# Heads of a sliding-window attention: scores and maxima twelve steps ahead of the exponentials instead of ten

## The chip, the cores and the metric

The kernel runs on one core of one Trainium2 chip. The metric is the device time of one execution in microseconds (us), the median of three runs. A core has a matrix engine (TensorE, PE in the profile; its weight loads are PEld), VectorE (DVE), ScalarE (ACT), GpSimd (POOL) and SyncE (SP), which here issues every DMA, in order. Matrix products land in PSUM, eight banks of 512 fp32 columns on 128 partitions.

## The reference, cut to what matters

Four layers, attention, Fourier mixing, attention, Fourier mixing, each on the normalised running sum `x` (2048 rows, 640 columns). The change touches the two attention layers alone:

```python
H = 32; Dh = D // H; W = 256
qkv = (x @ wqkv).reshape(B, S, 3, H, Dh).transpose(2, 0, 3, 1, 4)
q, k, v = qkv[0], qkv[1], qkv[2]
scores = einsum("bhqd,bhkd->bhqk", q, k) * (Dh ** -0.5)
mask = (idx[:, None] - idx[None, :] >= 0) & (idx[:, None] - idx[None, :] < W)
p = softmax(where(mask, scores, -1e9), axis=-1)
o = einsum("bhqk,bhkd->bhqd", p, v)
return o.transpose(0, 2, 1, 3).reshape(B, S, D) @ wo
```

A query sees its own block of 128 keys and the two before it, so a block row of scores is at most 384 wide.

## The kernel before, in words

**Before the heads** (`before_heads`, L368) the layer's rows are normalised and transposed, the value projections are made and stored, and the first two of ten column chunks of the query and key projection are done. A chunk is 128 columns: 6 or 7 heads' worth of rows of either kind. The other eight chunks are made *inside* the head loop, as filler for PE.

**The head loop** (`heads`, L606) walks 32 heads as 8 quads of 4 heads, each with 16 blocks of 128 queries: 128 steps. In a loop step three stages stand at different places of this sequence:

- `s = step + LEAD`: *scores and maxima*. `s_head` (matmul L631, DVE reduction L636) makes one block row of scores for one head and takes its masked row maximum, four times a step. Every fourth `s`, `m_rows` (L641) transposes the maxima of four blocks (PE, L644), negates them on ACT into `mt` (L647), and two DMAs (L649) write them as an extra row of `qp`.
- `t = step`: *exponentials*. `t_pair` (L659) makes the transposed scores again, now with the extra row, so that the maximum is already subtracted; `t_exp` (ACT, L669) takes the exponential and `t_mask` (POOL, L675 and L679) cuts the corners.
- `v = step - 1`: *values*. `pv` (L694) multiplies by V, three key blocks of four heads, and ACT copies the result out (L701). Every fourth `v`, `finish` (L705) posts, so many half steps later: the DMA that gathers the row sums (`sm`, L711), the store of the output rows (`o_d`, L712), the DVE reciprocal (L714) and the store of the reciprocals (`r_d`, L717).

A half step is one turn of the loop `for z in range(2)`; `post(delay, ...)` counts those. PSUM banks 0 to 3, and from step -1 also 4 and 5, go round among the three stages (`ring6`); 6 and 7 belong to the filler.

**The filler** is `fill(n)` (L752), which draws about `n` units from `project` (L568), a unit being two matmuls L257 of 512 columns that run side by side on two halves of the rows. 480 units are to be made in each layer. With `lead` on (steps below -2) and up to step -1 the filler is called in both half steps, `FIRST` units each; later once a step, `RATE` = 4 units. A piece of 128 by 512 results takes 15 units with its partner: pieces are made in sets of two banks, a first half of the rows and then the other half, and between the halves DVE reads a column of both banks (`seen`, L263) so that no two row halves write a bank at once. When a set is finished, ACT copies its banks out (L544), POOL splits the copy into two parts, and a DMA (L524) stores them in `qk_d`. In the leading steps a chunk is made as one group of four banks, 6, 7, 4 and 5, two sets side by side, and the copies are called at once.

After the last chunk the filler makes the first part of the output projection (`partials`, L954) out of chunks of `o_d` and `r_d` that `load_o` (L839) fetches and scales: 16 row blocks, some 18 units each, `LATE` = 9 units a step. `load_y` (L949) fetches the rows of `x` that are added.

**Order of the loads.** `due` (L726) holds for each quad `q` and quarter `j` the `s` at which `pack` (L582) is called; its twelve DMAs (L594, `kp` and `qp` from `qk_d`, 80 KB each) go out three a step over four steps. SP issues in program order, and a DMA that has to wait holds up all behind it. Loads are therefore counted from `s`, the finishing of quads and the filler's second part from `v` and `t`.

Of the kernel before, what the change touches and what calls it, by code (L numbers as in the profile page):

```python
# [21 lines left out]
NQ = H // 4  # L22
# [4 lines left out]
SCALE = DH ** -0.5  # L27
EPS = 1e-5

LEAD = 10  # L30
AHEAD = 8
EARLY = 3
AHEAD_X = 4
AFTER = 4
RATE = 4
FIRST = 7
LATE = 9
BACK = 2
PACE = 0.65
# [25 lines left out]
class Net:  # L65
# [501 lines left out]

    def project(self):  # L568
        for c in range(2, NCH):
            lead = self.lead  # L570
            for sbs in ((0, 1, 2, 3),) if lead else ((0, 1), (2, 3)):
                if sbs[0] == 0 and c > 2:
                    self.load_chunk(c + 1)
                if sbs[-1] == 3:
                    self.cut_chunk(c + 1)
                if c == NCH - 1:
                    self.prepare(sbs[0])
                yield from self.pieces(c, sbs, "f" if lead else "m")
        self.prepare(4)
# [26 lines left out]
    def heads(self, xsrc, xdst, hook):  # L606
# [78 lines left out]
        def pv(quad, qb, bank):  # L685

            bk, at = qb // 4, qb % 4 * P
            if qb % 4 == 0:
                ous[quad, bk] = self.next("ou")
            for kb in range(max(qb - 2, 0), qb + 1):  # L690
                t = pt[quad, kb]
                vq = self.vq[(4 * quad + kb // 4) % 3]
                for h in range(4):
                    nc.tensor.matmul(  # L694
                        self.banks[32 * h:32 * h + 32, bank, :P],
                        vq[:, 96 * (kb % 4) + 21 * h:96 * (kb % 4) + 21 * h + 32],
                        t[:, h, (qb - kb) * P:(qb - kb + 1) * P],
                        start=kb == max(qb - 2, 0), stop=kb == qb,
                        tile_position=(0, 32 * h), skip_group_check=True)
            pt.pop((quad, qb - 2), None)  # L700
            nc.scalar.activation(ous[quad, bk][:, at:at + P], self.banks[:, bank, :P], AF.Copy)  # L701
            if qb % 4 == 3:
                finish(quad, bk)

        def finish(quad, bk):  # L705
            ou = ous.pop((quad, bk))
            sm = pool.tile([P, 16], F32, name="sm", tag="sm")
            rc = pool.tile([P, 16], F32, name="rc", tag="rc")
            cols = slice(bk * 512, (bk + 1) * 512)
            at = (2, 9, 11) if quad < NQ - 1 else (1, 5, 6)  # L710
            self.post(at[0], lambda: nc.sync.dma_start(sm, ou[0:P:32, :]))  # L711
            self.post(at[0], lambda: nc.sync.dma_start(  # L712
                self.od[4 * quad:4 * quad + 4, :, cols].rearrange("h r s -> (h r) s"), ou))
            self.post(at[1], lambda: nc.vector.reciprocal(out=rc, in_=sm))  # L714

            def store():
                nc.sync.dma_start(  # L717
                    self.rd[bk, 4 * quad:4 * quad + 4, :].rearrange("h (a b) -> (h a) b", b=16), rc)
                self.post(2 if quad < NQ - 1 else 0, lambda: self.stored.add((quad, bk)))
            self.post(at[2], store)  # L720
# [55 lines left out]
        self.ring6 = dict.fromkeys((0, 1, 2, 3), -99.0)  # L776
        for step in range(-LEAD, steps + 1):
            now[0] = self.step = step
            clock = step * STEP
            if step == -1:  # L780
                self.ring6.update({4: -99.0, 5: -99.0})
            if step + LEAD == steps + 1:
                for b in ROLES["w"]:
                    self.ring6.pop(b, None)
            self.wide, self.lead, self.tiled = step + LEAD > steps, step < -2, step < steps - 1
            for f in later.pop(step, []):
                f()
            s, t, v = step + LEAD, step, step - 1
            if due and s >= due[0][0]:
# [9 lines left out]
            if done[0] < total:  # L799
                nf = max([FIRST if t < -2 else RATE + (t < 0)]  # L800
                         + [(d - done[0]) / max(1, at - s) for at, d, _, _ in due])
# [37 lines left out]
    def load_o(self, o, sb, k, raw=None, rr=None):  # L839
# [46 lines left out]

        busy = self.step + LEAD < 16 * NQ
        n, lane, eng = (2, "pool", nc.gpsimd) if busy else (1, "dve", nc.vector)
# [977 lines left out]
```

## Time and profile before

| | |
|---|---|
| median of three runs | 2188.04 us (2186.35 to 2188.07) |
| the profiled execution, whole | 2187.93 us |
| its span, first to last instruction | 2186.2 us |
| head loop of the first attention layer | about 125 to 530 us of the span |
| head loop of the second | about 1217 to 1619 us |
| PE, DVE, ACT, POOL busy over the span | 97%, 73%, 52%, 44% |

The page gives sums over the whole program; the head loops are two fifths of it, so stretches of them are read by the view that sums busy time in windows. The number of instructions L669 in a window tells how many steps it holds, two for each. A granted PE clock of 1.00 is full speed. PE's share of busy time says little there: ends of matmuls are modelled, and a waiting matmul can look long.

### The profile page before, as it was taken

To read this page: it belongs to the slowest core of one execution; us is meant where nothing else is said; L and a number is where in the kernel's file an instruction comes from. 1 tells how busy PE (TensorE), PEld (TensorE's weight loads), DVE (VectorE), ACT (ScalarE), POOL (GpSimd) and SP (SyncE) were. 2 spreads that over 40 slices of the span, in tenths; PEclk is the share of its full clock that TensorE was granted. 3 is DMA by queue.
4 is the path that set the end of the run, shared out by engine and by line. 5 is a ranking of instruction groups with operands and counts; after the bars stand their busy time and mean duration, and the time that the engine had idled before them with its cause. 6 is when DMAs were issued, how large, how long until landed. Compare 5 with 4: busy or idle time off the path is not lost.

```text
span 2186.2 us, 48927 instructions
## 1 busy us (share of the span) xinstructions
PE 2118.1 (97%) x17872; PEld 1783.2 (82%) x17872; DVE 1603.7 (73%) x3931; ACT 1140.5 (52%) x2125; POOL 958.0 (44%) x1562
## 2 busy tenths in 40 slices
PE   7999999988999999999999999999899999999999
PEld 7987777677878888889999877776778888888899
DVE  6358888886897868786661588888767968677676
ACT  3117777656554545452341177777565645445332
POOL 3037776765614222322430377767655033231324
PEclk9999999999999999999999999999999999999999
DMA  5546666785555354656645556567855454546653
GB/s 183 175 157 190 198 180 215 211 224 169 202 192 189 127 183 141 214 177 207 207 156 167 162 186 200 181 212 226 216 161 182 140 182 132 174 152 208 222 165 125
DMA packets 227089, 398.40 MB, mean 182 GB/s; under 512 B 39969, under 2 KB 86561, under 8 KB 226849
## 3 DMA queue, kind: packets, MB, share of 16 engines
q1 hardware_dynamic: 226848, 395.28, 57.3%
q8 instruction: 141, 2.31, 0.5%
q14 instruction: 100, 0.81, 0.1%
HBM read 273.94 MB, written 120.06 MB: 180 GB/s over the span
## 4 chain that ended last, share of the span: by engine, by line
PE 78%; DVE 7%; DMA 5%; ACT 4%; issue 3%; POOL 2%; SPq 1%; ACTq 0%; DVEq 0%; POOLq 0%
PE banks L1416 29%; PE banks L239 15%; PE banks L257 12%; PE banks L694 6%; PE banks L659 5%; PE banks L1704 5%; PE banks L631 5%; DMA qp<-qk_d 2%; DVE banks L636 1%; ACT pt L669 1%; DMA x_d<-x 1%; PE banks L341 1%; DMA kp<-qk_d 1%; ACT big L1039 1%; DVE qp L232 1%
## 5 line engine op out<-in xcount | busy, mean ns | idle before, releaser
L636 DVE CUSTOM_DVE_ANT_0 banks<-banks,mask 128x384 f32<-128x384 f32 (+2 forms) x1024 | 527.6, 557 | 123.0 <-PE banks L631 99.9
L669 ACT ACTIVATE pt<-banks 128x768 f32<-128x768 f32 (+2 forms) x512 | 393.8, 772 | 168.7 <-PE banks L659 55.2
L675 POOL TENSOR_SCALAR_AFFINE_SELECT pt<-pt 128x256 f32<-128x256 f32 x512 | 213.3, 417 | 213.8 <-ACT pt L669 192.0
L257 PE MATMUL banks<-big,wc 64*128 64x512 f32 x1920 | 271.1, 394 | 0.4 <-DVE pt L442 0.4
L659 PE MATMUL banks<-qp,kp 61*128 61x384 f32 (+2 forms) x1024 | 210.2, 381 | 22.8 <-DVE mc L636 17.4
L694 PE MATMUL banks<-pt,vq 128*32 128x128 f32 x5760 | 211.6, 278 | 3.5 <-ACT pt L669 3.4
L631 PE MATMUL banks<-kp,qp 60*128 60x384 f32 (+2 forms) x1024 | 205.5, 347 | 6.7 <-DVE mc L636 3.1
L257 PEld LDWEIGHTS banks<-big,wc 64*128 64x128 f32 x1920 | 186.8, 185 | 22.6 <-ACT x L544 1.5
L679 POOL TENSOR_SCALAR_AFFINE_SELECT pt<-pt 128x256 f32<-128x256 f32 x448 | 193.8, 433 | 0.0
L226 ACT ACTIVATE qp<-pt 128x512 fp32r<-128x512 f32 (+1 forms) x200 | 123.2, 625 | 128.1 <-DVE pt L1347 51.7
L232 DVE TENSOR_TENSOR qp<-pt,qp 128x512 fp32r<-128x512 f32 (+1 forms) x198 | 156.6, 798 | 42.1 <-ACT qp L226 40.5
L694 PEld LDWEIGHTS banks<-pt,vq 128*32 128x32 f32 x5760 | 142.4, 110 | 51.5 <-issue 35.3
L659 PEld LDWEIGHTS banks<-qp,kp 61*128 61x128 f32 x1024 | 108.0, 184 | 87.3 <-DVE mc L636 65.2
L1416 PE MATMUL banks<-qp,big 128*128 128x512 f32 x648 | 152.9, 390 | 0.0
L631 PEld LDWEIGHTS banks<-kp,qp 60*128 60x128 f32 x1024 | 123.6, 186 | 31.9 <-DVE mc L636 16.4
L1345 POOL TENSOR_TENSOR pt<-pt,pt 128x512 f32<-128x512 f32 x32 | 47.2, 1475 | 231.4 <-DMA pt<-c 173.4
L226 ACT ACTIVATE c<-pt 128x512 fp32r<-128x512 f32 x146 | 90.4, 625 | 111.1 <-POOL pt L1325 57.1
L636 DVE DVE_READ_ACCUMULATOR2_ANT mc<- 128x1 f32 x1024 | 145.0, 142 | 0.0
L1416 PEld LDWEIGHTS banks<-qp,big 128*128 128x128 f32 x648 | 120.8, 188 | 24.2
L232 DVE TENSOR_TENSOR c<-pt,c 128x512 fp32r<-128x512 f32 x144 | 113.8, 793 | 26.9 <-ACT c L226 24.4
L1416 PE MATMUL banks<-qp,xc 128*128 128x512 f32 x480 | 117.4, 391 | 4.3 <-DVE xc L232 2.8
L552 POOL CAST c<-x 128x512 fp32r<-128x512 f32 x64 | 38.9, 611 | 166.5 <-ACT x L544 162.3
(253 smaller groups left out, 4479.9 us busy)
## 6 DMA issues: line engine op xcount, KB each, us to landing
pt<-c SPq DMA_DIRECT2D x166, 512.0 KB
qk_d<-c SPq DMA_DIRECT2D x80, 512.0 KB
kp<-qk_d SPq DMA_DIRECT2D x384, 80.0 KB
qp<-qk_d SPq DMA_DIRECT2D x384, 80.0 KB
kp<-u_d SPq DMA_DIRECT2D x32, 640.0 KB
o_d<-ou SPq DMA_DIRECT2D x64, 256.0 KB
x_d<-x SPq DMA_DIRECT2D x48, 320.0 KB
v_d<-pt SPq DMA_DIRECT2D x16, 768.0 KB
```

The source lines that it names most:

```text
L226: nc.scalar.activation(hi, src, AF.Copy, scale=-1.0 if neg else 1.0)
L232: (eng or nc.vector).tensor_tensor(out=lo, in0=src, in1=hi.bitcast(F32), op=OP.subtract)
L239: self.nc.tensor.matmul(p, x, y, start=n == 0, stop=n == last)
L257: self.nc.tensor.matmul(ps[a], x[r], y[r], start=half + i == 0, stop=half == 1 and i == n - 1, skip_group_check=True)
L631: nc.tensor.matmul(p, qp[quad % 2][b:b + 60, z, qb * P:(qb + 1) * P], kp[quad % 2][b:b + 60, z, k0 * P:(qb + 1) * P], start=True, stop=True)
L636: nc.vector.tensor_tensor_reduce(out=p, in0=p, in1=self.mask[:, 384 - n * P:], scale=1.0, scalar=NEG, op0=OP.add, op1=OP.max, accum_out=mc ...
L659: nc.tensor.matmul(self.banks[:, banks[e], :n * P], kp[quad % 2][b:b + 61, z, kb * P:(kb + 1) * P], qp[quad % 2][b:b + 61, z, kb * P:(kb + ...
L669: nc.scalar.activation(pt[quad, kb][:, 2 * z:2 * z + 2, :n * P], self.banks[:, b0:b1 + 1, :n * P], AF.Exp, scale=SCALE)
L675: nc.gpsimd.affine_select(out=t[:, :, 0:P], in_=t[:, :, 0:P], pattern=[[0, 2], [1, P]], compare_op=OP.is_ge, fill=0.0, base=0, channel_mul ...
L679: nc.gpsimd.affine_select(out=t[:, :, 256:384], in_=t[:, :, 256:384], pattern=[[0, 2], [-1, P]], compare_op=OP.is_gt, fill=0.0, base=0, ch ...
L694: nc.tensor.matmul(self.banks[32 * h:32 * h + 32, bank, :P], vq[:, 96 * (kb % 4) + 21 * h:96 * (kb % 4) + 21 * h + 32], t[:, h, (qb - kb) ...
L1416: nc.tensor.matmul(self.banks[:, bk, :], p, b[q], start=start and m == 0, stop=stop and last and m == 2, skip_group_check=True)
```

## The change

Four edits, of numbers and conditions alone.

```diff
-LEAD = 10
+LEAD = 12
-FIRST = 7
+FIRST = 5
...
     def project(self):
         for c in range(2, NCH):
-            lead = self.lead
+            lead = self.lead and c == 2
             for sbs in ((0, 1, 2, 3),) if lead else ((0, 1), (2, 3)):
...
-            at = (2, 9, 11) if quad < NQ - 1 else (1, 5, 6)
+            at = (1, 5, 6) if quad == NQ - 1 else (2, 9, 11) if (quad, bk) == (NQ - 3, 0) else (2, 12, 14)
```

The loop starts at step -12 and the scores run twelve steps ahead of the exponentials; the ten leading steps with `lead` on take some 10 units each, where eight took 15. By the program's own counting the projection stands at 235 units at step 0, against 255, and ends with step 96 instead of step 91. The partials begin one step later (98 against 97) and fourteen of them are done by step 126 against 125; at the loop's end both stand alike. Only chunk 2 is made as a group of four banks; chunk 3, made in the lead as well, goes by sets of two on banks 6 and 7. Reciprocals and their stores are posted 12 and 14 half steps behind `finish` instead of 9 and 11, but for the last quad and one quarter of the sixth, which keep theirs.

What this moves, first on ACT from the start of the head loop of the first attention layer (`wc` are split weights of the next chunk, `x` the copied-out projections, `mt` the negated maxima). Before:

```order
L219 ACTIVATE wc<-x 128x384
L219 ACTIVATE wc<-x 128x256
L544 ACTIVATE x<-banks 128x512 x4
L219 ACTIVATE wc<-x 128x384
L219 ACTIVATE wc<-x 128x256
L647 ACTIVATE mt<-banks 16x128
L544 ACTIVATE x<-banks 128x512 x4
L647 ACTIVATE mt<-banks 16x128
```

And now, up to the first exponentials:

```order
L219 ACTIVATE wc<-x 128x384
L219 ACTIVATE wc<-x 128x256
L544 ACTIVATE x<-banks 128x512 x2
L647 ACTIVATE mt<-banks 16x128
L544 ACTIVATE x<-banks 128x512 x2
L647 ACTIVATE mt<-banks 16x128
L544 ACTIVATE x<-banks 128x512 x2
L219 ACTIVATE wc<-x 128x384
L219 ACTIVATE wc<-x 128x256
L669 ACTIVATE pt_95<-banks 128x768
L544 ACTIVATE x<-banks 128x512
```

The third pair of copies (step -4) empties banks 6 and 7 while the next set, which needs the same two banks, is the very next filler.

In the steady steps ACT's `mt` copy changes place against the pairs of L544. Before, steps 10 and 11 of the same layer:

```order
L669 ACTIVATE pt_97<-banks 128x768 x2
L701 ACTIVATE ou_99<-banks 128x128
L647 ACTIVATE mt<-banks 16x128
L669 ACTIVATE pt_98<-banks 128x768
L544 ACTIVATE x<-banks 128x512
L669 ACTIVATE pt_98<-banks 128x768
L544 ACTIVATE x<-banks 128x512
L701 ACTIVATE ou_99<-banks 128x128
```

Now, step 8:

```order
L701 ACTIVATE ou_100<-banks 128x128
L669 ACTIVATE pt_95<-banks 128x768
L544 ACTIVATE x<-banks 128x512
L669 ACTIVATE pt_95<-banks 128x768
L544 ACTIVATE x<-banks 128x512
L701 ACTIVATE ou_100<-banks 128x128
L647 ACTIVATE mt<-banks 16x128
```

The maxima go out at steps 0, 4, 8 where they went at 2, 6, 10, so that every second time they share the step with both copies of a set.

Last, SP where the first quarter of the last quad is loaded (`kp_104` and `qp_105` from `qk_d`; `big` are rows of `x`, `x<-o_d` and `rr` chunks for the partials). Before, from step 96:

```order
L594 DMA kp_104<-qk_d 20x2x512 x3
L952 DMA big_5880<-x 128x640
L859 DMA x<-o_d 128x1x512
L865 DMA rr_103<-r_d 128x1x512
L859 DMA x<-o_d 128x1x512
L711 DMA sm<-ou_100 128x1x16
L712 DMA o_d<-ou_100 128x512
L717 DMA r_d<-rc 128x16
L594 DMA qp_105<-qk_d 20x2x512 x3
```

Now, from step 94:

```order
L594 DMA kp_104<-qk_d 20x2x512 x6
L717 DMA r_d<-rc 128x16
L594 DMA qp_105<-qk_d 20x2x512 x3
L621 DMA vq_93<-v_d 128x384
L649 DMA qp_106<-mt 2x4x128 x2
L594 DMA qp_105<-qk_d 20x2x512 x3
L952 DMA big_6085<-x 128x640
L711 DMA sm<-ou_100 128x1x16
L712 DMA o_d<-ou_100 128x512
```

The loads of that quarter now all stand ahead of the fetches for the partials; those of the next quarter have the fetches among them.

## The prediction

> **What bounds the kernel now.** I read the page first, then the two head loops by windows, then how many steps each window holds, last the waits inside.
>
> ```profile
> span 2186.2 us, 48927 instructions
> PE 2118.1 (97%) x17872; PEld 1783.2 (82%) x17872; DVE 1603.7 (73%) x3931; ACT 1140.5 (52%) x2125; POOL 958.0 (44%) x1562
> ```
>
> The profiled execution took 2187.93 us, 1.7 more than its span and 0.1 under the median of 2188.04; sums below start from 2187.93. PE looks full over the whole program, so I ask stage by stage. Windows of the head loops (columns: length, busy us and count of PE, PEld, DVE, ACT, POOL, clock, DMA share, GB/s): the eight leading steps, steps -2 and -1, the steady steps, and the same for the second attention layer.
>
> ```profile
> 125.50:156.50 31.00, 30.81 (x275) 25.45 (x277) 19.21 (x73) 4.24 (x9) 11.54 (x17) 1.00 0.43 138
> 156.50:161.30 4.80, 4.80 (x44) 3.71 (x42) 3.90 (x14) 1.35 (x3) 3.47 (x6) 1.00 0.67 239
> 161.30:413.50 252.20, 247.78 (x3491) 188.04 (x3489) 209.89 (x786) 184.81 (x337) 184.52 (x423) 1.00 0.64 196
> 1217.40:1247.90 30.50, 30.50 (x275) 26.41 (x273) 19.35 (x73) 4.25 (x10) 11.60 (x17) 1.00 0.44 140
> 1247.90:1252.60 4.70, 4.70 (x42) 3.61 (x42) 3.84 (x14) 1.35 (x3) 3.42 (x6) 1.00 0.66 242
> ```
>
> In the lead PE has no idle time and DVE, at 19 of 31, has plenty: the lead is PE's. Its inside, from the timeline of PE:
>
> ```profile
> 148.63 0.34 PE L631 MATMUL banks<-kp,qp 60*128 60x384 f32 x2
> 148.81 1.99 PE L257 MATMUL banks<-big,wc 64*128 64x512 f32 x16
> 150.64 0.34 PE L631 MATMUL banks<-kp,qp 60*128 60x384 f32 x2
> 150.82 1.77 PE L257 MATMUL banks<-big,wc 64*128 64x512 f32 x14
> 152.42 0.34 PE L631 MATMUL banks<-kp,qp 60*128 60x384 f32 x2
> ```
>
> A half step with 8 units (16 matmuls) and two scores takes 150.64 - 148.63 = 2.01, one with 7 units 1.78. So a unit costs 0.23 us and two scores 0.17. A step of 15 units is 3.79.
>
> Then the steps after the lead, by exponentials (ACT L669, busy us and count; two make a step):
>
> ```profile
> 161.30:413.50 252.20, 143.12 (x184) 1.00 0.64 196
> 413.50:428.50 15.00, 6.38 (x10) 0.79 0.68 212
> 428.50:502.00 73.50, 32.74 (x42) 1.00 0.79 217
> 502.00:523.05 21.05, 11.21 (x14) 1.00 0.51 154
> 523.05:527.05 4.00, 2.58 (x4) 1.00 0.63 199
> 1252.60:1504.80 252.20, 143.18 (x184) 1.00 0.63 197
> 1504.80:1518.00 13.20, 6.41 (x10) 1.00 0.81 251
> 1518.00:1591.20 73.20, 32.74 (x42) 1.00 0.82 215
> 1591.20:1612.05 20.85, 11.32 (x14) 1.00 0.40 121
> 1612.05:1616.05 4.00, 2.58 (x4) 1.00 0.64 201
> ```
>
> Steady steps, 3.75 units on average: 252.2 / 92 = 2.74. Five steps without any filler (projection done, partials not ready): 13.2 / 5 = 2.64 in the second layer. So four units, 0.92 us of PE work, cost a step 0.1: the filler hides under the chain of scores, DVE maxima and banks. Steps with 9 units and scores: 73.2 / 21 = 3.49; with 9 and no scores 20.85 / 7 = 2.98; with neither 2.0. **A unit is dear in the lead and nearly free in the middle**, and that is the difference the change works on.
>
> **The change part by part.**
>
> *Lead.* Before, the ten steps below 0 took 31.0 + 4.8 = 35.8 and 30.5 + 4.7 = 35.2. Their work is 135 units (120 to 255) and 20 pairs of scores: 31.05 + 3.4 = 34.45; some 1.05 is left over for the start and the two transposes of the maxima. Now 115 units and 24 pairs: 26.45 + 4.1 + 1.05 = 31.6. DVE does not become the bound:
>
> ```profile
> 125.50:161.30 35.80, 20.23 (x77) 1.00 0.46 151
> ```
>
> That is all L636 work of the lead, 40 scores at 0.51, or 2.0 us a step against 2.64 for 10 units and four scores on PE.
>
> Against it stands chunk 3 on two banks. Its second set starts in the half step after its first ends, and must wait for both copies.
>
> ```profile
> L544 ACT ACTIVATE x<-banks 128x512 f32<-128x512 f32 x24 | 14.4, 600 | 0.1
> L647 ACT ACTIVATE mt<-banks 16x128 fp32r<-16x128 f32 x23 | 5.8, 252 | 0.1
> L669 ACT ACTIVATE pt<-banks 128x768 f32<-128x768 f32 (+2 forms) x184 | 143.1, 778 | 52.0 <-PE banks L631 18.3 <-POOL pt L675 17.8 <-PE banks L659 9.3
> ```
>
> Two copies are 1.2, less the 0.17 of scores that PE has meanwhile: 1.0. Two changes of row halves wait for DVE's column read between half steps, from nothing to two reductions (1.0) each. Taken 0.15 each, since DVE is idle a quarter of the time; the ends are 0 and 3.0 for all of it. The copies before stood behind other banks and cost nothing. Lead now 31.6 + 1.3 = 32.9: **-2.6 a layer, -5.2 in all** (ends -7.8 and -1.8).
>
> *Middle.* By the second layer: before 252.2 + 13.2 + 73.2 + 20.85 + 4.0 = 363.45. Now 97 steps of 2.74, one empty with scores, 18 of 3.49, ten of 2.98, one of 2.0: 265.8 + 2.6 + 62.8 + 29.8 + 2.0 = 363.0. The twenty units that left the lead fill five steps that were empty, which costs 0.1 a step; two steps of 9 units lose their scores, which pays for it. **-0.5 a layer, -1.0.**
>
> *The clock.* The first layer's empty steps took 15.0, the second's 13.2.
>
> ```profile
> 421.00:429.00 8.00, 7.27 (x72) 4.96 (x72) 5.35 (x20) 3.98 (x10) 4.01 (x8) 0.58 0.81 269
> 1512.00:1520.00 8.00, 7.27 (x107) 5.03 (x98) 6.95 (x26) 4.64 (x11) 5.04 (x11) 1.00 0.94 296
> ```
>
> Same place, same code, but a clock of 0.58 in the first. The stretch is where PE has least to do, and it shrinks from five steps to one. I take the drop as gone: **-1.8** (ends -2.3, the whole difference of the two layers' middles, 365.75 - 363.45, and 0).
>
> [...]
>
> *DMA waits.* Idle before an instruction of PE stands in brackets:
>
> ```profile
> 432.08 0.45 PE L659 MATMUL banks<-qp,kp 61*128 61x384 f32 x2 [1.08 <-DMA qp<-mt]
> 446.68 0.29 PE L631 MATMUL banks<-kp,qp 60*128 60x128 f32 x1 [1.00 <-DMA kp<-qk_d]
> 1536.29 0.29 PE L631 MATMUL banks<-kp,qp 60*128 60x128 f32 x1 [2.05 <-DMA qp<-qk_d]
> ```
>
> The first is a step whose exponentials waited for the maxima; two more steps between them make that wait go. The other two are the first scores of the last quad, whose loads stood behind the fetches for the partials; now they are issued ahead of them. The loads of the quarter behind get the fetches instead, so half is taken: 4.1 in all, **-2.0** (ends -4.1 and, a like wait for the quarter behind, +4.1).
>
> *Crowding and reciprocals.* Two more groups, of the whole program:
>
> ```profile
> L701 ACT ACTIVATE ou<-banks 128x128 f32<-128x128 f32 x256 | 71.5, 279 | 61.2 <-PE banks L694 49.9 <-DMA kp<-qk_d 0.4
> L714 DVE RECIPROCAL rc<-sm 128x16 f32<-128x16 f32 x64 | 15.9, 248 | 2.7 <-DMA sm<-ou 2.7
> ```
>
> Maxima, the finishing of a quarter and the first loads of a pack now begin in the same step, every fourth. ACT in a steady step has 2 x 0.78 + 0.28, a step with a set's copies 3.0, and with `mt` besides 3.3 against a step of 2.74. If the extra 0.25 shows each time (12 sets a layer) it is +6; if two delays that stood apart overlap, as much comes back. ACT is busy 185 of 252, so most of it is absorbed: taken **+2** (ends -6 and +6).
>
> The reciprocals cost 248 ns each, as many as before, and DVE waits 2.7 us for their sums in the whole program; they are moved behind a later phase of the same queue. The store of a quarter's reciprocals is wanted only by the fetches for the partials, and the one that the first partial waits for keeps its delays: nothing.
>
> Sum: -5.2 - 1.0 - 1.8 - 2.0 + 2.0 = -8.0, or **2179.9**.
>
> **The rivals.**
>
> *The clock drop stays* (0.12): all else as above, -6.2, 2181.7.
>
> *The lead's gain is eaten* (0.22): set changes cost 3.0 a layer instead of 1.3 (+3.4), the last quad's loads wait as before (+2), crowding takes 2 more and the clock stays low half the time: about -1, 2187. For it: in the lead a set change has no step of pv and exponentials to hide under. Against it: DVE and ACT are far from full there.
>
> *Slower by crowding* (0.16): one mechanism, in every fourth steady step. The transpose of the maxima holds PE's queue, and pv, the scores and all filler stand behind it. In the lead such a half step takes 1.76 us (157.53 to 159.29) where its neighbour takes 1.32:
>
> ```profile
> 157.53 0.34 PE L631 MATMUL banks<-kp,qp 60*128 60x384 f32 x2
> 159.29 0.34 PE L631 MATMUL banks<-kp,qp 60*128 60x384 f32 x2
> 160.61 0.34 PE L631 MATMUL banks<-kp,qp 60*128 60x384 f32 x2
> ```
>
> That is 0.44 for maxima that now share the step with a set's copies and the start of the loads. If 0.3 more is lost in each of 24 such steps in each layer, that is +14.4, and -8.0 becomes +6.4: 2194. It decides from 8.0 / 48 = 0.17 us a step.
>
> *Everything overlaps* (0.12): crowding gives back 4 instead of taking 2: 2174.
>
> **How the numbers follow.** The forecast itself has 0.38, its own range 2176.5 to 2183.5. A measurement of this kernel can tell about 0.2%, 4.4 us, from no change. The forecast, the staying clock and the overlap are faster by more: 0.62. The eaten gain is the same: 0.22. Crowding is slower: 0.16. The range reaches down to a little under the overlap and up to half of the slower case: 2172 to 2190.
>
> **What would show it.** The lead's window would be 32 to 34 us from the first scores to step 0, with PE gaps of about a microsecond at one set change behind ACT L544. The five steps without filler would shrink to one, with the clock at 1.00 in the first layer too. The waits of 1.0 and 2.05 before the last quad's first scores would be smaller. Steady steps would stay at 2.70 to 2.78; at 2.85 or more, with waits for ACT or for DVE at every fourth step, the crowding rival is right. A lead of 35 us would refute the first term, and with it the prediction.

## The result, and the profile after

The changed kernel takes **2192.75 us** (median of 13 runs, 2189.99 to 2197.61) against 2186.7 for the kernel before in the same session: 1.0029 times as long, 95% interval 1.0019 to 1.0039. It is slower by 0.3%, where the prediction had 2179.9 and faster. The profiled execution took 2191.20 us, 3.3 more than the 2187.93 of before.

The page's head says nothing of where: every engine is as busy as before, within 2.2 us.

```profile
span 2189.5 us, 48888 instructions
PE 2117.7 (97%) x17872; PEld 1783.6 (81%) x17872; DVE 1603.3 (73%) x3931; ACT 1139.1 (52%) x2125; POOL 955.8 (44%) x1562
```

Windows of the changed kernel, first the twelve leading steps of each layer, then the steady steps (length, busy us and count of PE, PEld, DVE, ACT, POOL, clock, DMA share, GB/s):

```profile
125.60:160.60 35.00, 33.22 (x283) 26.47 (x283) 27.34 (x102) 4.38 (x10) 12.31 (x18) 1.00 0.51 167
1216.35:1250.75 34.40, 32.77 (x281) 25.80 (x278) 27.36 (x102) 4.38 (x10) 12.31 (x18) 1.00 0.52 169
160.60:411.99 251.39, 246.66 (x3495) 187.26 (x3496) 210.13 (x785) 183.72 (x335) 183.05 (x420) 1.00 0.63 192
```

The lead was 35.8 and 35.2 and is 35.0 and 34.4; PE, which had no idle time in it, now has 1.7 us. The 92 steady steps were 252.2 and are 251.4.

Now the stretches behind, by exponentials (L669, two to a step): twelve steps, **one step**, thirteen steps, for each layer.

```profile
412.00:448.27 36.27, 18.02 (x24) 1.00 0.81 235
448.27:459.21 10.94, 1.62 (x2) 0.69 0.74 216
459.21:503.32 44.11, 19.80 (x26) 1.00 0.75 202
1502.35:1539.93 37.58, 18.02 (x24) 0.95 0.86 238
1539.93:1550.83 10.90, 1.62 (x2) 0.69 0.73 220
1550.83:1594.84 44.01, 19.80 (x26) 1.00 0.70 196
```

Step 104 holds two exponentials like any other and takes 10.9 us, three times its neighbours' time, in both layers. In the kernel before the same step took 4.0 (all engines, first and second layer):

```profile
453.92:457.94 4.02, 2.62 (x46) 2.17 (x46) 3.81 (x11) 1.89 (x5) 3.50 (x7) 1.00 0.56 163
1543.51:1547.52 4.01, 2.62 (x46) 2.17 (x46) 3.81 (x11) 1.89 (x4) 3.50 (x7) 1.00 0.65 193
```

PE's timeline of the changed kernel in the second layer says why:

```profile
1539.39 0.45 PE L659 MATMUL banks<-qp,kp 61*128 61x384 f32 x2 [0.30 <-DVE mc L636]
1541.36 0.41 PE L631 MATMUL banks<-kp,qp 60*128 60x384 f32 x1 [1.52 <-DMA qp<-qk_d]
1544.75 0.66 PE L631 MATMUL banks<-kp,qp 60*128 60x384 f32 x1 [2.98 <-DMA qp<-qk_d]
```

Scores (L631) wait twice for a load of `qp`. Step 104 is where `s` reaches 116, the second quarter of the last quad, so these are the loads that now have the fetches among them. The first layer has the same two waits, of 1.97 and 2.98. What stands on SP at that time (start, duration of the issue or issues; between them SP waits):

```profile
1525.86 0.35 SPq L952 DMA_DIRECT2D big<-x_d  x1
1526.25 1.36 SPq L594 DMA_DIRECT2D kp<-qk_d  x3
1528.65 0.52 SPq L859 DMA_DIRECT2D x<-o_d  x1
1529.36 0.60 SPq L865 DMA_DIRECT2D rr<-r_d  x1
1530.34 0.35 SPq L717 DMA_DIRECT2D r_d<-rc  x1
1531.73 0.39 SPq L524 DMA_DIRECT2D qk_d<-c  x1
1533.69 0.33 SPq L952 DMA_DIRECT2D big<-x_d  x1
1534.07 1.13 SPq L594 DMA_DIRECT2D qp<-qk_d  x3
1535.49 0.34 SPq L621 DMA_DIRECT2D vq<-v_d  x1
1536.01 1.16 SPq L952 DMA_DIRECT2D big<-x_d  x1
1537.26 0.38 SPq L524 DMA_DIRECT2D qk_d<-c  x1
1537.73 2.67 SPq L649 DMA_DIRECT2D qp<-mt  x2
1540.45 1.22 SPq L594 DMA_DIRECT2D qp<-qk_d  x3
```

The two triples of `qp` belong to steps 100 and 101 and go out in steps 102 and 104. Ahead of them stand loads of rows of `x` (L952, 320 KB each), fetches for the partials (L859, L865) and stores of the last chunk (L524). And SP's own waits there:

```profile
SPq L952 <- DMA big<-x_d: 2.4, 2, 1.6
SPq L649 <- DMA big<-x_d: 1.5, 1, 1.5
```

`big` is a row block of `x`. L649 stores maxima and needs no row of `x`; yet it waits for one to land. The load it waits for is that of 1533.69, eight issues ahead of it; the load that the L952 of 1533.69 waits for is that of 1525.86, again eight ahead. All 1922 DMA issues of this trace report their landing to eight semaphores in turn, 240 or 241 issues to each. Each of the 1914 issues that have one eight before them began only when that one had landed, 222 of them within 0.1 us of it: here **an issue waits until the one eight before it has landed**. The rows of `x` in this list took 7.8, 6.1 and 6.1 us to land, and at the eighth issue behind each of the first two SP stood still until it had, 1.6 and 1.5 us.

The wait has a tail: the clock falls to 0.5 for 6.8 us inside it (at 450.4 and 1542.65 us), which is the 0.69 of those windows. Two stretches of it, all engines, the clock behind POOL:

```profile
1542.00:1543.00 1.00, 0.00 (x0) 0.00 (x0) 0.43 (x2) 0.00 (x0) 0.34 (x1) 0.82 0.59 188
1543.00:1544.00 1.00, 0.00 (x0) 0.00 (x0) 0.00 (x0) 0.00 (x0) 0.00 (x0) 0.50 0.88 256
```

### The profile page after: what moved, and what is told of

Its sections match the earlier page's. It is cut to its first block, busy times and chain, and to the rows that moved or that the text cites. A ratio compares the mean times of both kernels' runs of the same rounds, so it can differ in the third digit from the quotient of the medians.

```text
span 2189.5 us, 48888 instructions
## 1 busy us (share of the span) xinstructions
PE 2117.7 (97%) x17872; PEld 1783.6 (81%) x17872; DVE 1603.3 (73%) x3931; ACT 1139.1 (52%) x2125; POOL 955.8 (44%) x1562
## 3 DMA queue, kind: packets, MB, share of 16 engines
q8 instruction: 141, 2.31, 0.4%
## 4 chain that ended last, share of the span: by engine, by line
PE 75%; DVE 9%; DMA 6%; ACT 4%; issue 3%; POOL 3%; SPq 2%; ACTq 0%; DVEq 0%; POOLq 0%
PE banks L1416 29%; PE banks L239 15%; PE banks L257 11%; PE banks L694 5%; PE banks L1704 5%; PE banks L659 5%; PE banks L631 4%; DVE banks L636 2%; DMA kp<-qk_d 1%; DMA big<-x_d 1%; ACT pt L669 1%; SPq L594 1%; PE banks L341 1%; DVE qp L232 1%; ACT big L1039 1%
## 5 line engine op out<-in xcount | busy, mean ns | idle before, releaser
L669 ACT ACTIVATE pt<-banks 128x768 f32<-128x768 f32 (+2 forms) x512 | 393.5, 770 | 193.2 <-PE banks L659 109.1
L257 PE MATMUL banks<-big,wc 64*128 64x512 f32 x1920 | 278.3, 396 | 3.6 <-DVE seen L263 1.9
L659 PE MATMUL banks<-qp,kp 61*128 61x384 f32 (+2 forms) x1024 | 209.5, 380 | 23.7 <-DVE mc L636 17.7
L631 PE MATMUL banks<-kp,qp 60*128 60x384 f32 (+2 forms) x1024 | 205.7, 346 | 11.1 <-DMA qp<-qk_d 9.5
L257 PEld LDWEIGHTS banks<-big,wc 64*128 64x128 f32 x1920 | 186.5, 186 | 29.4 <-DVE seen L263 3.6
L659 PEld LDWEIGHTS banks<-qp,kp 61*128 61x128 f32 x1024 | 108.7, 185 | 87.0 <-DVE mc L636 59.0
L631 PEld LDWEIGHTS banks<-kp,qp 60*128 60x128 f32 x1024 | 122.0, 187 | 33.7 <-DMA qp<-qk_d 6.5
```

The source lines that it names most:

```text
L257: self.nc.tensor.matmul(ps[a], x[r], y[r], start=half + i == 0, stop=half == 1 and i == n - 1, skip_group_check=True)
L631: nc.tensor.matmul(p, qp[quad % 2][b:b + 60, z, qb * P:(qb + 1) * P], kp[quad % 2][b:b + 60, z, k0 * P:(qb + 1) * P], start=True, stop=True)
L659: nc.tensor.matmul(self.banks[:, banks[e], :n * P], kp[quad % 2][b:b + 61, z, kb * P:(kb + 1) * P], qp[quad % 2][b:b + 61, z, kb * P:(kb + ...
L669: nc.scalar.activation(pt[quad, kb][:, 2 * z:2 * z + 2, :n * P], self.banks[:, b0:b1 + 1, :n * P], AF.Exp, scale=SCALE)
```

## The experiments

The theory after the result (A): the projection now ends five steps later, and its end starts the loads of `x` and soon the fetches. The first four rows used to go out in steps 93 to 96, ahead of the last quad's loads; now the rows share steps 97 to 103 with these loads, in one queue. From SP's timeline in the kernel before, second layer (rows of `x`, L952, and stores of the last chunk, L524):

```profile
1508.11 1.15 SPq L952 DMA_DIRECT2D big<-x_d  x2
...
1510.55 0.39 SPq L524 DMA_DIRECT2D qk_d<-c  x1
...
1514.37 0.80 SPq L952 DMA_DIRECT2D big<-x_d  x2
1515.27 0.38 SPq L524 DMA_DIRECT2D qk_d<-c  x1
```

Its rivals (B): the transfers are late because the DMA engines are full there, in whatever order; or the wait belongs to the twelve steps ahead. All ratios are to the kernel before, timed in the same session.

**The last quad's first two quarters two steps earlier.**

```diff
-        due = [(16 * q + 4 * j - AHEAD + 2 * (q == NQ - 1),
+        due = [(16 * q + 4 * j - AHEAD + 2 * (q == NQ - 1 and j > 1),
```

> The changed kernel, with the loads of the last quad's first two quarters called two steps earlier (at s = 104 and 108 instead of 106 and 110), nothing else. In the changed kernel step 104 of both attention layers takes 10.9 us, where PE waits 1.5 and 3.0 us for qp rows of the last quad's second quarter and is idle some 7 in all. Theory 1 (order in SP's queue: these q loads stand behind the rows of x and the chunks for the partials, and every DMA issue waits for the one eight issues before it): the q loads now stand ahead of most of these fetches, step 104 falls to 3 to 4 us in both layers, and the time to 2177 to 2182, about 11 to 15 us under the changed kernel and 5 to 9 under the kernel before. Rival (the twelve-step lead and the crowding of the fourth step are the cost, the wait only shows them): the idle time moves to another step and the time stays within 3 us of the changed kernel's 2192.75.

2187.95 us, ratio 1.0006 (0.9997 to 1.0015), between the two times expected. Step 104 falls to 4.3 and 4.1 us; steps 99 and 100 rise to 5.0 and 4.9 (5.4 and 4.8 in the second layer) from 3.5 and 3.4, and step 112 to 4.9 and 7.2 from 4.1. The same bytes in another order take the ratio from 1.0029 to 1.0006, some 5 us: order matters, and what is left moves to other places of the same queue.

**Two rows of `x` ahead of the partials instead of four** (`AHEAD_X = 2`).

> The changed kernel with two instead of four blocks of x rows fetched ahead of the partials (AHEAD_X = 2), so that two 320 KB loads fewer stand in SP's queue ahead of the last quad's second-quarter q loads. Theory 1 (the queue): step 104 falls from 10.9 by 3 to 6 us in each layer, time 2181 to 2188, unless a partial then waits for its rows. Second theory (SP is held by the stores of the last projection chunk, which wait for POOL, and not by the fetches): step 104 stays above 9.5 and the time within 3 us of 2192.75.

2191.65 us, 1.0019 (1.0009 to 1.0029). Step 104 takes 9.3 and 9.7 us. Two rows fewer in the burst take 1.6 and 1.2 us out of the wait, less than the 3 to 6 of theory 1; the time is the second theory's.

**Chunk 3 as a group of four banks again**, with banks 4 and 5 given to the head loop at step 2 instead of -1.

```diff
-            lead = self.lead and c == 2
+            lead = self.lead and c <= 3
...
-            if step == -1:
+            if step == 2:
```

> The changed kernel, but chunk 3 too is made as a group of four banks, and banks 4 and 5 join the ring of the three stages at step 2 instead of -1. It tells what the set change on banks 6 and 7 costs in the lead (the steps from -5 to -2 take 3.0, 3.1, 5.05 and 2.85 us in the changed kernel against 2.65 where nothing changes). If the set change is the cost: these steps fall to 2.65 to 2.75 each, but for the transposes' 0.4 in one, some 2.7 us less a layer, with up to 1 us more in steps 0 and 1 for want of two banks; time 2187 to 2191. If the lead is held by DVE or by the transposes: the steps keep their lengths and the time stays at 2192 to 2195. Step 104 stays at 10 to 11 us under either.

2195.17 us, 1.0033 (1.0022 to 1.0044). The lead shrinks by 0.6 us a layer, but step -6 now stalls (5.2 us) and steps 0 and 1 take 3.6 and 3.3 us (3.5 and 2.6 in the changed kernel), by this reading for want of banks: no gain. Step 104 stays long, 14.4 and 10.8. The place of the stall moves with the banks.

**The old delays of the reciprocals** (`at` as before the change, the rest changed).

> The changed kernel with the reciprocals and their stores posted as before the change (9 and 11 half steps behind the finishing of a quarter instead of 12 and 14). It prices this edit alone. If the edit does nothing, as predicted: within 2 us of the changed kernel. If the later posts are what keeps DVE or SP from waiting for the sums in the new phase: slower than the changed kernel by 3 us or more, with more idle time of DVE before L714 than the 2.7 us of the kernel before. If the later stores are part of what blocks SP at step 104: faster by 3 us or more.

2193.9 us, 1.0027 (1.0015 to 1.0040), indistinguishable from the changed kernel; step 104 stays long (12.2 and 13.8). The reciprocals cost and bring nothing that shows.

**Loads of `x` issued by ACT.**

```diff
-                self.nc.sync.dma_start(self.y_part(t), ...
+                self.nc.scalar.dma_start(self.y_part(t), ...
```

> The changed kernel with the loads of the rows of x (L952) issued by ACT instead of SP; the same bytes at about the same places. Theory A, the new wait of some 7.5 us at step 104 is one of order: SP issues in program order with about eight transfers outstanding, and long loads of x hold back the loads of the last quad behind them. Then step 104 falls from 10.9 us to 3.3 to 4.5, and the kernel to 2177 to 2183 us. Rival B, the DMA engines are full in this stretch (8 to 9 tenths busy) and the loads would be late in any order: step 104 stays at 9 us or more and the time at 2190 to 2194. A third way: ACT itself is held by its issues, with waits of exponentials; then steps 96 to 104 grow by 0.3 us each, and the kernel takes 2185 to 2190.

2220.79 us, 1.0152 (1.0137 to 1.0167): much worse, and by none of the three accounts. Step 104 stays at 11.7 and 12.0, step 100 takes 7.1 and 10.0 and step 112 10.5 and 10.8. ACT is hardly held by its issues, 0.33 us each and one of 0.89 in this stretch. SP is, from one row of ACT's timeline and SP's waits:

```profile
1532.89 0.34 ACTq L952 DMA_DIRECT2D big<-x_d  x1
```

```profile
SPq L711 <- DMA big<-x_d: 3.4, 1, 3.4
SPq L594 <- DMA big<-x_d: 3.4, 2, 2.2
```

SP waits 6.8 us for loads that it did not issue, ahead of L711 and L594, which read no row of `x`: by this reading the DMAs of both engines share the eight semaphores. So this edit did not take the rows out of the chain; it only let them start outside SP's queue and close together, six between 1532.89 and 1542.51 us, and it cannot decide between A and B. Bandwidth alone does not explain it either: the DMA engines are 0.66 to 0.81 busy in the 20 us in which SP waits.

**Rows of `x` cut to 32 columns**, the partial sums stored without `x` (so the addition is left out); every transfer keeps its place.

```diff
-                self.nc.sync.dma_start(self.y_part(t), self.xsrc[t * P:(t + 1) * P, :])
+                self.nc.sync.dma_start(self.y_part(t)[:, :32], self.xsrc[t * P:(t + 1) * P, :32])
...
-            nc.vector.tensor_tensor(out=y, in0=self.banks[:, b0:b0 + 2, :320], in1=y, op=OP.add)
+            nc.vector.tensor_copy(out=y, in_=self.banks[:, b0:b0 + 2, :320])
```

> The changed kernel with each load of a row block of x cut from 640 to 32 columns and the partial sums stored without adding x, so a part of the computation is left out; all transfers keep their number and their places in SP's order. If the long landings of the rows of x cause the wait at step 104 (by order or by bytes), it falls from 10.9 us to 3 to 5. If the fetches for the partials and the stores of the last chunk cause it, it stays above 8.

Step 104 falls to 7.4 and 5.7 us, with one wait in place of the two (second layer):

```profile
1536.54 0.41 PE L631 MATMUL banks<-kp,qp 60*128 60x384 f32 x1 [1.60 <-DMA qp<-qk_d]
```

One run of 2182.07 us. SP has no wait for `big` left, the longest of any kind is 0.5 us. The long landings of `x` are most of the new wait, 3.5 and 5.2 of some 7 us. The rest belongs to the other transfers in the queue, and which of them was not separated.

**All four quarters two steps earlier, two rows ahead** (the extra 2 taken out of `due`, `AHEAD_X = 2`).

> The changed kernel with all four quarters of the last quad loaded two steps earlier (the extra 2 in the due table taken out) and two rows of x loaded ahead instead of four. Theory A (order): the waits at steps 104 and 112 both go, and what came back at steps 99 and 100 (3 us in all with two quarters alone) shrinks with the fewer loads of x: 2183 to 2187 us. Rival B (full DMA engines): the wait only moves to other steps between 97 and 112, the same sum, 2188 to 2192.

2189.64 us, 1.0018 (1.0005 to 1.0032): by size the rival's. Step 104 is back at 7.8 and 6.7. In the second layer the first load of the third quarter now stands right behind a store of the last chunk, which it reads, and SP waits 4.0 us there for that store to land.

**Less projection in the lead alone, ten steps ahead** (the kernel before with `FIRST = 5`, chunk 3 by sets of two).

> The kernel before with one edit of the change alone, less projection work in the lead (FIRST 5, one group of four banks), scores ten steps ahead as before, reciprocals as before. The projection then ends at step 101 instead of 91. If it is the later end of the projection that puts the fetches and loads of x among the loads of the last quad, a new wait of 5 us or more shows at one of the steps 104 to 112 (step 104 took 4.0 before), and the kernel takes 2190 to 2200 us. If the wait of the changed kernel came from the twelve steps ahead, no such wait shows, and the shorter lead (27 us instead of 35) less the work pushed to the end leaves 2178 to 2185.

2218.84 us, 1.0145 (1.0130 to 1.0159), worse than either expected. This order changes what is computed too (why is not known), so only its times are read. The lead is 28.2 and 27.6 us, and there is a long wait with ten steps ahead as well: step 103 takes 10.6 and 11.0. It is another wait than that of step 104, though. DVE stands 7.6 us (8.0 in the second layer) at the addition of the first partial, for its row of `x`, and holds the maxima behind it:

```profile
454.46 0.82 DVE L978 TENSOR_TENSOR big<-banks,big 128x640 f32<-128x640 f32 x1 [7.61 <-DMA big<-x]
```

Steps 89 and 90 take 6.2 and 5.1, where they took 3.0 and 2.8. So a later end of the projection (step 100 here) brings a long wait for DMA without twelve steps ahead; that it brings the wait of step 104 is not shown by this run.

**The projection's end put back**, by a fifth unit in each step from 72 on.

```diff
-                nf = max([FIRST if t < -2 else RATE + (t < 0)]
+                nf = max([FIRST if t < -2 else RATE + (t < 0 or t >= 72)]
```

> The changed kernel with five units of filler a step instead of four from step 72 on, so that the projection ends near step 91 as it did before the change; everything else, the twelve steps ahead and the short lead among it, is the change's. The rows of x are then loaded in steps 91 to 93 and not among the loads of the last quad. Theory A (the later end of the projection puts the loads of x and the fetches among the last quad's loads): step 104 falls from 10.9 us to 3.3 to 4.5, the twenty steps from 72 cost up to 0.1 us more each, and the kernel takes 2176 to 2181 us. Rival: the wait belongs to the twelve steps ahead and the order of the last quad's own loads; then step 104 stays above 8 us and the time at 2190 or more.

2190.09 us, 1.0002 (0.9989 to 1.0015): the time is the rival's, step 104 is theory A's. Windows of it: the twenty steps from 72 in the second layer, then step 104 of the second and of the first layer.

```profile
1446.33:1507.01 60.68, 59.55 (x811) 45.12 (x810) 48.08 (x174) 43.29 (x80) 46.87 (x100) 1.00 0.66 204
1545.34:1549.80 4.46, 3.76 (x55) 3.01 (x56) 3.61 (x10) 2.04 (x5) 3.33 (x7) 1.00 0.82 183
453.62:458.05 4.43, 3.73 (x55) 3.01 (x56) 3.61 (x10) 2.04 (x5) 3.33 (x7) 1.00 0.78 193
```

and the same twenty steps of the changed kernel (ACT's L669 alone), then the projection's matmuls (L257, PE and PEld) in these steps, of this kernel and of the changed one:

```profile
1446.30:1502.35 56.05, 31.09 (x40) 1.00 0.62 195
```

```profile
1446.33:1507.01 60.68, 26.41 (x186) 18.57 (x186) 1.00 0.66 204
1446.30:1502.35 56.05, 22.25 (x150) 14.90 (x152) 1.00 0.62 195
```

The wait is gone, with twelve steps ahead and the short lead untouched: this is theory A. But the twenty steps cost 60.7 - 56.05 = 4.6 us for (186 - 150) / 2 = 18 more units, 0.26 each, where 0.1 a step was expected. **The fifth unit of a step is as dear as one in the lead (0.23)**; only the first four were cheap.

**The kernel before with the last quad's first two quarters earlier** (the first edit of this section on the kernel before).

> The kernel before, with the first two quarters of the last quad loaded two steps earlier, that is in the order against the fetches that the change gave them, and nothing else. Theory: this alone takes the waits of 1.0 and 2.05 us at the first scores of the last quad, 3 us in all, and 2183 to 2185 us result, since the rows of x are loaded in empty steps here. Rival: the next quarter, moved up into the fetches, waits instead as in the changed kernel, with one of the steps 102 to 106 at 6 us or more and 2188 or more.

1.0012 (0.9997 to 1.0027, median 2193.55), no gain. The two waits of before do go (step 102: 3.5 and 3.9), but step 97 takes 6.1 and 6.8, on another tile:

```profile
1523.60 0.69 PE L659 MATMUL banks<-qp,kp 61*128 61x384 f32 x2 [3.94 <-DMA qp<-mt]
```

Exponentials wait for their maxima, whose store stands behind the moved loads. With ten steps ahead that store has two steps less until it is wanted. Twelve ahead do not bring a gain by themselves; by this reading they are what lets the last quad's loads go first.

**The changed kernel with the first two quarters earlier and two rows ahead.**

> The changed kernel with the first two quarters of the last quad loaded two steps earlier (which gave 2187.95 by itself) and two rows of x loaded ahead instead of four. If SP's queue in steps 97 to 101 is what costs, the stalls of 1.5 to 2 us each that came at steps 99 and 100 shrink, and the kernel takes 2183 to 2186; if the fetches and not the rows of x hold that queue, it stays at 2187 to 2190.

2186.38 us, 0.9989 (0.9973 to 1.0004). The stalls at steps 99 and 100 do not shrink (5.0 and 4.9; 5.0 and 4.8). DVE shows what they are:

```profile
1526.50 0.82 DVE L978 TENSOR_TENSOR big<-banks,big 128x640 f32<-128x640 f32 x1 [1.74 <-DMA big<-x_d]
```

The first row of `x` is itself late, and DVE, waiting for it, holds the maxima behind it.

**With five units from step 84 besides.**

> The changed kernel with the first two quarters of the last quad loaded two steps earlier, two rows of x ahead, and five units of filler a step from step 84 on, which ends the projection about two steps earlier. In the kernel without the last of these the steps 99 and 100 still lose 3.5 us a layer, because DVE waits for the first row of x, which stands behind the late queue. Theory (the queue of SP decides): the row is loaded two steps earlier, both steps fall to 3.1 to 3.5 us, the ten steps from 84 cost up to 2.2 us a layer more (a fifth unit cost 0.2 us in the run with it from step 72), and the kernel takes 2182 to 2186 us. Rival: the stalls at steps 99 and 100 stay and the fifth units come on top, 2188 to 2191.

2188.58 us, 0.9998 (0.9986 to 1.0010). Steps 99 and 100 are at 3.5, as expected, and the fifth units cost about 1.3 us a layer (0.85 in steps 80 to 92, 0.45 in 92 to 97); step 112 of the second layer waits again (7.5). The time is the rival's.

**The split of chunk 4's weights four half steps later**, on the changed kernel, for the lead.

```diff
-                    self.cut_chunk(c + 1)
+                    self.post(4, lambda: self.cut_chunk(4)) if c == 3 else self.cut_chunk(c + 1)
```

The lead of the changed kernel stalls in step -3 (5.05 us against 2.65, counted by DVE's maxima, four to a step). First PE, then DVE in the first layer:

```profile
151.57 1.91 PE L257 MATMUL banks<-big,wc 64*128 64x512 f32 x10 [0.57 <-ACT x L544]
...
157.29 1.43 PE L257 MATMUL banks<-big,wc 64*128 64x512 f32 x10 [0.96 <-DVE seen L263]
```

```profile
154.63 1.53 DVE L211 TENSOR_TENSOR wc<-x,wc 128x384 fp32r<-128x384 f32 x2
157.08 0.15 DVE L263 COPY seen<-banks 128x2 f32<-128x2 f32 x1
```

> The changed kernel with the split of the weights of chunk 4 posted four half steps later, so that DVE's two splits (1.53 us together, step -3) no longer stand ahead of the column read at the change of row halves, for which PE waits 0.96 us. Theory: these splits took what the lead did not give; step -3 falls from 5.05 us to 3.0 to 4.1 and the lead from 34.4 to 32.9 to 33.6 in the second layer, 2 us in all. Rival: the set change on the two banks itself costs it (PE waits for ACT's copies 0.57 us, and the scores' banks after it), or the split only stalls a later step; then the lead stays at 34.2 or more.

The lead becomes 34.1 and 33.5 us, step -3 3.86:

```profile
124.04:158.13 34.09, 33.21 (x283) 26.29 (x283) 26.16 (x100) 4.38 (x10) 12.02 (x18) 1.00 0.52 169
1217.34:1250.81 33.47, 32.73 (x283) 25.86 (x279) 26.16 (x100) 4.38 (x10) 12.03 (x18) 1.00 0.54 171
```

So the splits were half of what the lead lacks, 0.9 a layer. Steps -3 and -2 together still take 1.7 us more than two undisturbed ones; by this reading that is the set change, and PE's 0.57 for ACT is still there. The whole took 2192.8 us, 1.0015 (1.0004 to 1.0025), with the wait at step 104 untouched (12.1 and 11.6).

**The three edits together.**

> Both together: the last quad's loads, the rows of x and the fill of the one, the later split of the other. If the queue of SP and the lead's split are the two causes, this is faster than before the change: 2179 to 2184 us. If either only moves its stall, 2186 or more.

2186.82 us, 0.9991 (0.9980 to 1.0001): no gain over the kernel before, and in the range of a moved stall.

**The earlier quarters, two rows and the later split, without fifth units.**

> The changed kernel with the first two quarters of the last quad loaded two steps earlier, two rows of x ahead and the later split of chunk 4, without the fifth unit. If the gains add: 2186.4 (the first two) less the lead's 0.9 a layer, 2184 to 2185.5 us, 0.1 to 0.2 per cent under the kernel before. Rival: the 0.9 is given back at another wait, as when the split alone was moved, and the time stays at 2186 to 2188.

**2185.36 us, 0.9984 (0.9973 to 0.9996)**: the only version that computes the same and is under the kernel before by more than its interval, by 0.16%. One of fifteen, and by so little, it is weak evidence of a gain. The stalls at steps 99 and 100 are still in it (6.6 and 5.5; 7.3 and 4.3).

## Why the prediction was wrong, by its own steps

The two profiled executions differ by +3.3 us: 2191.20 against 2187.93. By stages, both layers summed, from first score to exponentials 0, 92, 100 and 127:

| stage | predicted | measured |
|---|---|---|
| lead | -5.2 | -1.6 |
| middle to step 92, with crowding | +1.0 | -1.4 |
| steps 92 to 100, with the clock | -1.8 | -0.5 |
| steps 100 to 127, the DMA waits | -2.0 | +10.3 |
| outside the head loops | 0 | -3.6 |

The prediction's -1.0 for the middle as a whole is in the second row; by its own count of steps most of it falls into the third. The last row is scatter: the stretch between the two head loops, where the code is the same, took 689.9 us before, 687.0 after, and between 686.7 and 690.9 in all the other kernels here but one. Without that row the head loops lost 6.8 us, near the 6.05 between the medians.

**DMA waits: the step that failed.** The prediction saw the right place and said that the quarter behind would get the fetches; it took half of 4.1 as saved, and gave the other end as "a like wait for the quarter behind, +4.1". The step lost about 6.9 us in each layer, clock included (10.9 against 4.0 for the same step before). It had priced the fetches alone, by a wait of before. What it left out is the end of the projection: it counted the five empty steps as fillable for 0.1 each, and did not see that in them SP was doing work, four rows of `x` and two stores of the last chunk. These moved with the projection's end into the last quad's loads. A kernel with the projection's end put back, by a fifth unit in twenty steps, has no such wait; with rows of 16 KB instead of 320 the step is 3.5 and 5.2 us shorter. The saving that it counted on did come: the first scores of the last quad, in step 102 before and in step 100 now, no longer wait, and their step takes 3.35 us in both layers against 4.60 and 5.74. With the end put back, steps 100 to 118 took 61.2 and 61.0 us against 62.9 and 63.5 before: 4.2 saved in both, the better end of this term (4.1). Why the rows take so long to land is not separated: the DMA engines were 0.81 and 0.86 busy in steps 92 to 103, against 0.63 in the steady steps, so full engines (B) may have a part in it.

**Lead: right in kind, mis-sized.** -0.8 a layer instead of -2.6. The prediction had a second set change at 1.0 and the column reads at 0.15 each, "since DVE is idle a quarter of the time". It is, but its two splits, 1.53 us together, stood ahead of one read, and PE waited 0.96 there; moving them gave 0.9 a layer. A lead of 35 us, which was to refute the term, is what came.

**Middle and crowding.** The rival "slower by crowding" is refuted: 92 steps take 251.4 and 251.6, 2.73 each. The cheap middle unit held as well, but only to four a step: a fifth cost 0.26.

**The clock.** The first layer's 12 steps from 92 on ran at 1.00, as said, but with the new wait came a drop, now in both layers. These two, 6.8 us at 0.5 each, begin 2.2 and 2.8 us (450.4 and 1542.65) after the last pair of L659 ends, with one score between. In the second layer another drop, of 3.4 us, came at 1518.8 us, in steps 97 and 98, where the kernel before had none; it is the 0.95 of that window. So steps 92 to 100 became 2.31 us shorter in the first layer and 1.85 longer in the second, and the row comes to -0.5 instead of -1.8. The kernel with the projection's end put back has the empty steps again, and there the drop came in the second layer (6.8 us at 1515.7) and not in the first. Which layer has such a drop is therefore not settled by these steps alone: the -1.8 was read from one execution. Why the first layer's empty steps had one before, where PE showed no such wait, stays open.

**Reciprocals.** Nothing, as predicted.

**The rivals.** "The lead's gain is eaten" adds up to +0.3, or 2188.2 (-8.0 + 3.4 + 2 + 2 + 0.9), and not to about -1, 2187. "Slower by crowding" gave 2194, near the measured time, by a mechanism that was not there.

## What to carry to other kernels

Stretches in which the matrix engine has little to do may be where a queue does its work: before filling them, list what every queue issues there and where that goes. When all DMAs go through one ordered queue, count its transfers and their bytes step by step around each load with a deadline, and look for long ones within as many issues ahead of it as there are semaphores to hand round, eight here. A price of filler taken at one rate (four units a step, 0.03 each) need not hold for the next unit, 0.26 here.

## What the runs showed that was not expected

- In the changed kernel, where SP alone issues, all 1914 issues that have one eight before them, with the same semaphore, came behind its landing. With ACT issuing the rows of `x`, SP waited 3.4 us at once for a row that ACT had issued: by this reading both draw on the same eight. Moving long loads to another engine's queue made the kernel 1.5% slower here.
- Six rows of `x`, 320 KB each, needed 3.5 to 7.8 us to land in steps 98 to 102 of the second layer (the 32 us from 1518 moved 240 GB/s), and SP's own issues took 0.3 to 1.2 us each.
